# Three fused layers on one core: both heads of a pair normed together, all K and Q casts on ScalarE, a new order

## The chip, the cores and the metric

The kernel runs on one core of a Trainium2 chip. The core has five engines with a queue each, and each works its queue strictly in order: PE (TensorE, matmuls; its weight loads are a row of their own, PEld), DVE (VectorE), ACT (ScalarE), POOL (GpSimd) and SP (which only starts transfers here). PE writes to PSUM, eight banks of 512 float32 columns in each of 128 partitions; DVE and ACT read PSUM, POOL does not. The metric is the device time in microseconds of one execution, and the median over several executions.

## The reference, cut to what matters

Attention over 4 batches, 8 heads, 576 tokens and 64 columns a head, each head's output mixed with a read from a memory matrix, followed by a mixture of experts (8 experts, 288 tokens each) and a last layer of three products and a maximum.

```
scores = q @ k.T / 8, causal mask, softmax with the row's maximum taken off
local  = softmax @ v
mem    = (phi(q) @ M_prev) / (phi(q) @ z_prev + 1e-6)
out    = g * mem + (1 - g) * local          # g = sigmoid(beta), one per head
x      = moe(out)                           # each token to one expert, experts have a capacity
y      = maximum of three x @ w, then @ w_out
```

Everything is float32. The softmax needs the sum of each row's exponentials; the kernel gets it as one more column of the product with v, and divides at the end.

## The kernel before, in words

The attention runs over 16 pairs of heads (four batches of four pairs), numbered from 0 here. For a pair, with K and Q loaded as `Kr` and `Qr`:

- *Casts and differences.* For each head `KX`, `QX` and `KB` are rounded copies of K and Q (`ck`, `cq`, `cb` in `pair`), which the scheduler may give to ACT or to DVE; POOL then subtracts them from the originals in pieces of 192 columns (L84), so that the product of rounded parts and remainders keeps float32 accuracy.
- *S* (L509) and *J* (L511): the scores with the queries in the partitions, only to get the row maximum. DVE reduces each piece (L528). J is the last block of 64 queries of both heads at once. *N* (L562) transposes the maxima, ACT copies them, and three small transfers put them into a row of `QL`.
- *T* (L629, L630): the scores again with the keys in the partitions, now with the maximum taken off, in four groups a head: 512 columns; 64 and 448; 320 and 192; and a 64x64 corner. ACT takes the exponential into `PT` (L640), POOL masks the diagonal blocks (L658).
- *AV* (L675): 15 products a head of `PT` with V, into one PSUM bank per head, `av_109` for the first head of each pair and `av_110` for the second. 73 columns a query block are used: 64 of output, 8 of the head's share of the expert gate, and the row's sum.
- *Norm* (`norm`, L693 to L704), on DVE for each head: the sums times the gate factor (`r`), their reciprocal, the product with the bank (`tmp`), and two additions into `x`, 320 and 40 columns a partition.
- *M* (L724) is the memory product of the pair and *G* (L407) the gate's product with V. Besides, 24 pieces of the last layer's weights are converted from 64-bit halves by ACT and DVE (L869 to L879).

The eight PSUM banks of this stage are two for AV, one for M, G and small products, three for S and two for T. The 64x64 corner of T has no bank of the T ring: it goes to the free columns 448 to 511 of the head's own AV bank, so it is written after the previous owner of that bank has been normed.

Nothing of the order is written by hand. Every step is a task with a key (a place in the program, shifted by the entries of `PRIO`), the engines that may do it with a guessed cost for each, its inputs and its buffers. `Plan.run` then plays the program through with those costs and sets the order in which each engine gets its instructions. The costs (`act`, `dve`, and numbers beside the tasks) are thus no times of the chip, but they decide the order. `FILL` sets 32 matmuls on constant data (L790, `warm`), which have the last key of all and go where PE would otherwise idle at the start; `COLD` is the time before which the planner counts PE's work twice.

After the attention comes the routing of the tokens (a chain of small steps between DVE and PE), and then the experts and the last layer, with a plan of their own.

Of the kernel before, what the change touches and what calls it, by code (L numbers as in the profile page):

```python
# [33 lines left out]
NJ = 5  # L34
# [97 lines left out]
class Plan:  # L132
# [113 lines left out]
def attention(g, tc, ctx, consts, beta, qT, kT, qN, v1, vT, mz, mT, wg, xd, L, m2):  # L246
# [97 lines left out]
    def pair(p):  # L344
# [103 lines left out]
        def head(i):  # L448
# [42 lines left out]
    def maxes(r, p):  # L491
# [5 lines left out]
        def piece(key, heads, j, a, z, first, last, dep):  # L497
# [19 lines left out]
            def fR(e):  # L517
# [4 lines left out]
                if not last:  # L522
# [81 lines left out]
    def unit(r, p, i):  # L604
# [14 lines left out]
        for gi, gr in enumerate(groups):  # L619
            o = K()  # L620
            bt = Buf(R["t"]) if gi < 3 else r.bav[i]

            def fT(e, gr=gr, o=o, gi=gi):
                o.t = ps.tile([128, 512], F32, name="t", bufs=BUFS["t"]) if gi < 3 else AV[h % 2][:, 448:512]
# [23 lines left out]
        for gi, (kb, cnt, st) in enumerate(((0, 2, 576), (2, 2, 320), (4, 1, 64))):  # L648
# [11 lines left out]

            c = {"DVE": dve(cnt * m), "POOL": 40 + 1.25 * cnt * m}
            mk.append(add(n1 + W["M"] + .1 * gi, {x: c[x] for x in W["maske"]}, fM, ex[:2] if gi == 0 else ex[2:3] if gi == 1 else ex[3:],
                          use=[bP]))
        out = []
        for j in range(NJ):
            m = rows(j)

            def fA(e, j=j, m=m):

                av = AV[h % 2][:, j * C:j * C + CA]  # L670
                for kb in range(j + 1):
# [7 lines left out]
                           mk[:1] + (fill if p == 0 else []) + (ex[1:2] if j else []) + (mk[1:2] if j > 1 else []) + (mk[2:] if j > 3 else []) + [r.tV] + out[-1:],  # L679
                           use=[bP, r.b["V"], r.bav[i]]))  # L680
        return out

    def norm(r, p, i, deps, mems):
        b, pp = divmod(p, H // 2)
        h = 2 * pp + i
        n = r.n + 5 * i + 4 + W["norm"]
        av = av3(AV[h % 2])
        u = K()
        br, bt = Buf(R["r5"]), Buf(R["tmp"])

        def f1(e):
            u.r5 = tile("r5", [128, NJ])
            V.tensor_scalar(u.r5, av[:, :, 72], 1.0e-9, g.c1[:, h:h + 1], op0=OP.add, op1=OP.mult)  # L693

        def f2(e):
            V.reciprocal(u.r5, u.r5)

        def f3(e):
            u.tmp = tile("tmp", [128, NJ, 72])
            V.tensor_mul(u.tmp, av[:, :, :72], u.r5[:, :, None].to_broadcast([128, NJ, 72]))  # L700

        def f4(e):
            for x, c0, c1 in ((x2s[b].t[:, :, h], 0, 64), (xs[b][:, :, h], 64, 72)):
                vg(e).tensor_add(x, x, u.tmp[:, :, c0:c1])  # L704

        t = add(n, {"DVE": 130}, f1, deps + [cdone], new=[br], use=[r.bav[i]])
        t = add(n + .1, {"DVE": 100}, f2, [t], use=[br])
        t = add(n + .2, {"DVE": dve(360)}, f3, [t], new=[bt], use=[br, r.bav[i]])
        c = {"POOL": 1020, "DVE": dve(320) + 90}
        return add(n + .3, {x: c[x] for x in (W["xadd"] if p < NP - 1 else ("POOL", "DVE"))}, f4, [t] + mems, use=[bt, r.bx, r.bx2])  # L710

    def mem(r, p, part):
# [30 lines left out]
        def f3(e):  # L743
# [3 lines left out]
            for dst, c0, c1 in ((x2s[b].t, 0, 64), (xs[b], 64, 72)):  # L747
# [74 lines left out]
    for p in range(NP):  # L822
# [24 lines left out]
    def conv(k):  # L847
# [728 lines left out]
```

## Time and profile before

| | us |
|---|---|
| median of 3 runs | 941.97 (934.69 to 942.91) |
| the profiled execution | 938.56, span 936.8 |
| attention, first instruction to the last norm | 0 to 296.5 |
| routing and start of the experts | 296.5 to 360 |
| experts and last layer | 360 to 936.8 |
| busy over the span: PE, DVE, ACT, POOL | 863.9, 570.9, 316.5, 433.6 |

The page is one execution on the chip. A busy PE there is an upper figure, since matmuls are pipelined and their ends are modelled. DMA issues of an engine are not counted as busy. Times in the rows below are us from the start of the span, unless ns is written.

### The profile page before, as it was taken

How to read it: one execution, taken by the hardware profiler on the slowest of the kernel's cores; microseconds unless marked ns; L12 is line 12 of the kernel's file. 1: busy time of each engine (PE TensorE's matmuls, PEld its weight loads, DVE VectorE, ACT ScalarE, POOL GpSimd, SP SyncE). 2: the span in 40 equal slices, each digit the busy share in tenths (PEclk: the TensorE clock that was granted, in tenths of full speed). 3: DMA queues.
4: the chain of work that ended last, by engine and by line, in shares of the span. 5: the costliest groups of instructions: out<-in, count | busy, mean ns of one | idle time of the engine just before them, and what ended most of it. 6: DMA issues, size and time to landing. Idle time of an engine off the chain costs nothing.

```text
span 936.8 us, 17494 instructions
## 1 busy us (share of the span) xinstructions
PE 863.9 (92%) x6493; PEld 788.0 (84%) x6493; DVE 570.9 (61%) x1708; ACT 316.5 (34%) x683; POOL 433.6 (46%) x665
## 2 busy tenths in 40 slices
PE   8999999999997467999989998999999999979997
PEld 5888888888886357989979988989998998979996
DVE  5699999997756864842682683484376386123121
ACT  3445555553334032223124133224223224322211
POOL 1758777677421396344064155136208326730301
PEclk9699999999998569999999999999999999989999
DMA  7456776854201122231042032024014114340000
GB/s 282 164 200 201 252 256 218 281 162 133 94 18 52 54 62 91 72 112 46 2 138 91 2 115 95 21 79 138 23 47 146 38 52 154 116 91 23 24 1 34
DMA packets 37601, 97.86 MB, mean 104 GB/s; under 512 B 9620, under 2 KB 9740, under 8 KB 37516
## 3 DMA queue, kind: packets, MB, share of 16 engines
q1 hardware_dynamic: 34240, 87.24, 28.8%
q0 software_dynamic: 2976, 9.44, 3.0%
q8 instruction: 51, 0.84, 0.4%
q14 instruction: 34, 0.28, 0.1%
q10 hardware_dynamic: 300, 0.07, 0.0%
HBM read 87.22 MB, written 9.45 MB: 103 GB/s over the span
## 4 chain that ended last, share of the span: by engine, by line
PE 61%; DVE 11%; POOL 10%; issue 8%; DMA 8%; ACT 2%; SPq 0%; POOLq 0%; ACTq 0%; DVEq 0%
PE av L675 10%; PE w L1323 7%; PE w L1325 7%; PE w L1324 7%; DMA wraw<-in_wr 5%; PE acc L1325 4%; PE acc L1323 4%; PE acc L1324 4%; POOL ml L84 4%; POOL wlo L84 3%; PE s L509 3%; PE t L629 2%; PE mem L724 2%; PE t L630 2%; PE mem L407 2%
## 5 line engine op out<-in xcount | busy, mean ns | idle before, releaser
L84 POOL TENSOR_TENSOR wlo<-wraw,whi 128x256 fp32r<-128x256 f32 x224 | 167.6, 783 | 253.2 <-ACT whi L1289 251.1
L1323 PE MATMUL w<-yh,mh 128*128 128x288 f32 x576 | 175.1, 304 | 4.8 <-ACT mt L1425 4.8
L1324 PE MATMUL w<-yl,mh 128*128 128x288 f32 x576 | 171.7, 298 | 0.1
L1325 PE MATMUL w<-yh,ml 128*128 128x288 f32 x576 | 171.1, 297 | 0.0
L675 PE MATMUL av<-V,PT 128*128 128x112 f32 (+2 forms) x960 | 130.7, 275 | 0.0
L675 PEld LDWEIGHTS av<-V,PT 128*128 128x128 f32 (+2 forms) x960 | 114.9, 174 | 13.7 <-issue 4.6
L1323 PEld LDWEIGHTS w<-yh,mh 128*128 128x128 f32 x576 | 109.9, 191 | 8.0 <-ACT mt L1425 5.0
L1324 PEld LDWEIGHTS w<-yl,mh 128*128 128x128 f32 x576 | 109.9, 191 | 3.4 <-DVE yl L1229 0.3
L1325 PEld LDWEIGHTS w<-yh,ml 128*128 128x128 f32 x576 | 110.1, 191 | 0.0
L1227 DVE SCALAR_TENSOR_TENSOR hl<-w,hh 128x288 fp32r<-128x288 f32 x64 | 28.8, 456 | 132.3 <-ACT hh L1221 132.3
L1427 DVE TENSOR_TENSOR mt<-w,mt 128x288 f32<-128x288 f32 x96 | 43.5, 453 | 102.9 <-PE w L1325 84.0
L1289 ACT CAST whi<-wraw 128x1024 fp32r<-128x1024 f32 x64 | 67.2, 1049 | 114.9 <-DMA wraw<-in_wr 89.9
L528 DVE CUSTOM_DVE_ANT_0 junk<-s,mask 128x256 bf16<-128x256 f32 (+4 forms) x145 | 72.8, 505 | 23.6 <-PE s L509 19.8
L1325 PE MATMUL w<-xhi,wlo 128*128 128x288 f32 x256 | 77.7, 304 | 8.1 <-DVE wlo L78 7.5
L640 ACT ACTIVATE PT<-t 128x512 f32<-128x512 f32 x96 | 54.5, 594 | 78.7 <-PE av L675 48.7
L1323 PE MATMUL w<-xhi,whi 128*128 128x288 f32 x256 | 78.0, 305 | 1.1 <-ACT whi L1289 1.1
L1324 PE MATMUL acc<-hl,whi 128*128 128x288 f32 x256 | 76.8, 300 | 0.8 <-DVE hl L1227 0.8
L1324 PE MATMUL w<-xlo,whi 128*128 128x288 f32 x256 | 77.1, 301 | 0.0
L1323 PE MATMUL acc<-hh,whi 128*128 128x288 f32 x256 | 77.1, 301 | 0.0
L1325 PE MATMUL acc<-hh,wlo 128*128 128x288 f32 x256 | 76.5, 299 | 0.0
L84 POOL TENSOR_TENSOR KX<-Kr,KX 64x192 fp32r<-64x192 f32 x90 | 63.1, 729 | 21.0 <-ACT KX L312 13.8
L658 POOL TENSOR_SCALAR_AFFINE_SELECT PT<-PT 128x256 f32<-128x256 f32 (+1 forms) x96 | 41.2, 440 | 66.7 <-ACT PT L640 61.2
(236 smaller groups left out, 1925.0 us busy)
## 6 DMA issues: line engine op xcount, KB each, us to landing
wraw<-in_wr SPq DMA_DIRECT2D x64, 512.0 KB
Kr<-in_kT SPq DMA_DIRECT2D x15, 576.0 KB
Qr<-in_qT SPq DMA_DIRECT2D x15, 576.0 KB
V<-in_v SPq DMA_DIRECT2D x16, 384.5 KB
m2raw<-in_m2w SPq DMA_DIRECT2D x12, 512.0 KB
QN<-in_qN SPq DMA_DIRECT2D x16, 288.0 KB
VT<-in_vT SPq DMA_DIRECT2D x16, 288.0 KB
xd<-x SPq DMA_DIRECT2D x16, 256.0 KB
```

Of the source, the lines that this page charges most:

```text
L84: u = nc.gpsimd.tensor_sub(o[:, c], a[:, c], b[:, c])
L509: nc.tensor.matmul(o.s[:, :z - a], r.QX[i][:, 128 * j:128 * j + 128], r.KX[i][:, a:z], start=True, stop=True)
L528: V.tensor_tensor_reduce(out=junk[ps_, :z - a], in0=o.s[ps_, :z - a], in1=mask[ps_, k:k + z - a], scale=-0.125, scalar=init, op0=OP.add, o ...
L640: A.activation(u.PT[:kr, at0:at0 + wd], o.t[:kr, :wd], AF.Exp, scale=0.125)
L658: G.affine_select(v, v, pattern=[[1, m]] if cnt == 1 else [[0, 2], [1, m]], compare_op=OP.is_ge, fill=0.0, base=0, channel_multiplier=-1)
L675: nc.tensor.matmul(av[:m], u.PT[:kr, o:o + m], r.Vw[:kr, c:c + CA], start=(kb == 0), stop=(kb == j))
L1227: V.scalar_tensor_tensor(lo(), src(), 0.0, hi().bitcast(F32), op0=OP.max, op1=OP.subtract)
L1289: A.copy(x.W[fb][0], x.RAW[fb])
L1323: nc.tensor.matmul(o, wh, rh, start=start, stop=False)
L1324: nc.tensor.matmul(o, wh, rl, start=False, stop=False)
L1325: nc.tensor.matmul(o, wl, rh, start=False, stop=stop)
L1427: V.tensor_max(q.mt, o.pt[:, :T], q.mt)
```

## The change

Three things in the attention; the routing, the experts and the last layer keep their code.

1. The two AV banks become one tile of two banks, and the two heads of a pair are normed together after both: five DVE instructions a pair where there were ten, with twice the columns. The two AV banks come free together. The ring of `tmp` goes from three buffers to two. The 64x64 corner of T goes to the T ring like the other groups.
2. From the second pair on, the casts to `KX`, `QX` and `KB` may only go to ACT.
3. The costs that the planner counts with, and several keys, are replaced, with `COLD` from 6000 to 25000; so each engine's order changes through the whole attention.

```diff
-PRIO = {..., 'phi': 2.0, ..., 'cpe': ['ACT', 'DVE'], ..., 'J4': -2.0, 'R': -78.0, ..., 'N': -37.5, 'T': -3.0, ..., 'gate': 45.5, 'G': -13.0, ...}
+PRIO = {..., 'phi': 22.0, ..., 'cpe': ['ACT'], ..., 'J4': 38.0, 'R': -98.0, ..., 'N': -42.5, 'T': -43.0, ..., 'gate': 2.5, 'G': -3.0, ...}
...
-NROW, COLD, NLAT = 1, 6000, 3000
+NROW, COLD, NLAT = 1, 25000, 3000
...
-    AV = [ps.tile([128, 512], F32, name=f"av{i}") for i in range(2)]
+    AVP = ps.tile([128, 2, 512], F32, name="av")
+    AV = [AVP[:, i] for i in range(2)]
...
     def act(n, psum=False):
-        return 22 + 0.89 * n if psum else 60 + 0.89 * n
+        return 135 + 0.89 * n if psum else 155 + 0.89 * n
...
-            bt = Buf(R["t"]) if gi < 3 else r.bav[i]
+            bt = Buf(R["t"])
...
-    def norm(r, p, i, deps, mems):
+    def norm(r, p, deps, mems):
+
         b, pp = divmod(p, H // 2)
-        h = 2 * pp + i
-        n = r.n + 5 * i + 4 + W["norm"]
-        av = av3(AV[h % 2])
+        h = slice(2 * pp, 2 * pp + 2)
+        n = r.n + 9 + W["norm"]
+        av = AVP[:, :, :NJ * C].rearrange("p i (j c) -> p j i c", j=NJ)
...
-            u.tmp = tile("tmp", [128, NJ, 72])
-            V.tensor_mul(u.tmp, av[:, :, :72], u.r5[:, :, None].to_broadcast([128, NJ, 72]))
+            u.tmp = tile("tmp", [128, NJ, 2, 72])
+            V.tensor_mul(u.tmp, av[:, :, :, :72], u.r5[:, :, :, None].to_broadcast([128, NJ, 2, 72]))
...
-        for i in range(2):
-            last = unit(r, p, i)
-            nm.append(norm(r, p, i, last, [m0, m1]))
+        last = unit(r, p, 0) + unit(r, p, 1)
+        r.avs = [r.bav[0], r.bav[1]]
+        nm.append(norm(r, p, last, [m0, m1]))
```

How the order moves, at two places. First ACT near the start, before: `c_120`, `c_121` are small constants, `QL<-t` the maxima of pair 0's first head, and `KX<-Kr` x2 the first casts of pair 1.

```order
L103 ACTIVATE c_120<-bt 128x8
L104 ACTIVATE c_121<-bt 128x8
L312 COPY V<-mem 128x10x8
L312 CAST QL<-t 1x512
L312 CAST QL<-t 1x64
L312 CAST KX<-Kr 128x576 x2
L640 ACTIVATE PT<-t 128x512
```

The casts of pair 1 stand behind three copies that wait for PE. The same place in the changed kernel:

```order
L103 ACTIVATE c_119<-bt 128x8
L104 ACTIVATE c_120<-bt 128x8
L310 CAST KX<-Kr 128x576
L310 CAST KB_126<-Kr 64x576
L310 CAST KX<-Kr 128x576
L310 CAST QX<-Qr 128x576 x2
L310 CAST KB_127<-Kr 64x576
L420 ACTIVATE ph<-QN 128x576
L425 ACTIVATE ph<-ph 128x576
L638 ACTIVATE PT<-t 128x512
```

Now all six casts of pair 1 and its `phi` stand directly behind the constants, and the three copies have gone to DVE.

Second, PE where pair 7 ends and pair 8 begins, before: `av_110` is the bank of a pair's second head, `av_109` that of the next pair's first.

```order
L675 MATMUL av_110<-V,PT 64x112 x5
L509 MATMUL s<-KX,QX 128x128
L675 MATMUL av_109<-V,PT 128x112
L509 MATMUL s<-KX,QX 128x256
L675 MATMUL av_109<-V,PT 128x112 x2
```

One S piece stands between the last product of a pair and the first of the next. The same place in the changed kernel, where both heads write the one tile `av`:

```order
L673 MATMUL av<-V,PT 64x112 x5
L509 MATMUL s<-KX,qj_129 128x512 x2
L509 MATMUL s<-KX,qj_129 128x64 x2
L627 MATMUL t<-QX,KX 128x320
L628 MATMUL t<-QL,KB_125 128x320
L627 MATMUL t<-QX,KX 128x192
L628 MATMUL t<-QL,KB_125 128x192
L627 MATMUL t<-QX,KX 64x64
L628 MATMUL t<-QL,KB_125 64x64
L673 MATMUL av<-V,PT 128x112 x2
```

Four J matmuls and three groups of T now stand between; the corner of T is written to `t`, no longer to the AV bank.

## Rows read from the trace of the kernel before

**Rows 1.** Windows: stretch, its length, busy us (xcount) of PE, PEld, DVE, ACT, POOL, clock, DMA.
```profile
28.00:45.00 17.00, 16.54 (x64) 14.68 (x65) 10.70 (x39) 8.10 (x19) 13.41 (x24) 0.51 0.39 132
...
75.00:200.00 125.00, 122.44 (x889) 106.37 (x888) 119.75 (x388) 66.79 (x143) 95.08 (x145) 1.00 0.72 237
200.00:287.00 87.00, 83.67 (x615) 72.71 (x616) 59.05 (x202) 34.08 (x74) 42.87 (x113) 1.00 0.27 84
```

**Rows 2.** One line's instructions, norm's product: duration ns min/median/max, first and last start.
```profile
L700 DVE TENSOR_TENSOR tmp<-av,r x32: 514/528/534, 49.5 to 295.3; 128x360 f32<-128x360 f32 x32
```

**Rows 3.** The chain that ended last, one pair late in the attention: start, length, what.
```profile
242.43 0.69 DVE junk L528
...
244.65 1.05 issue
245.70 0.58 DVE x L704
```

**Rows 4.** Waits of PE, 60 to 290: waiting, releaser, us in total, times, longest.
```profile
PE s L562 <- DVE nm L528: 3.4, 4, 1.0
```

**Rows 5.** Groups by shape, 0 to 310, norm and M's product: count | busy us, mean ns.
```profile
L704 DVE TENSOR_TENSOR x<-x,tmp 128x320 f32<-128x320 f32 x32 | 21.5, 672 | 0.3
L704 DVE TENSOR_TENSOR x<-x,tmp 128x40 f32<-128x40 f32 x32 | 11.6, 362 | 0.0
L748 DVE TENSOR_TENSOR x<-mem,rm 128x384 f32<-128x384 f32 x16 | 8.7, 547 | 0.2
L693 DVE TENSOR_SCALAR r<-av,c 128x5 f32<-128x5 f32 x32 | 7.1, 221 | 15.5 <-PE av L675 13.4 <-ACT mh L1200 2.0
L748 DVE TENSOR_TENSOR x<-mem,rm 128x256 f32<-128x256 f32 x16 | 6.6, 411 | 0.2
L696 DVE RECIPROCAL r<-r 128x5 f32<-128x5 f32 x32 | 5.9, 184 | 0.2
```

**Rows 6.** The same view: casts of K and Q on DVE, and one kind on ACT.
```profile
L312 ACT CAST QX<-Qr 128x576 fp32r<-128x576 f32 x19 | 12.8, 671 | 5.8 <-PE av L630 3.2 <-PE av L629 2.5
L312 DVE CAST KB<-Kr 64x576 fp32r<-64x576 f32 x19 | 11.3, 595 | 0.5 <-PE av L630 0.5
L312 DVE CAST QX<-Qr 128x576 fp32r<-128x576 f32 x13 | 7.1, 556 | 0.0
L312 DVE CAST KX<-Kr 128x576 fp32r<-128x576 f32 x13 | 6.2, 476 | 0.0
```

**Rows 7.** Timeline: an addition of norm beside POOL's subtraction: start, us, engine.
```profile
227.18 1.94 POOL L84 TENSOR_TENSOR QL<-Qr,QX 64x192 fp32r<-64x192 f32 x3 [0.60 <-PE av L630]
227.22 1.96 DVE L704 TENSOR_TENSOR x<-x,tmp 128x320 f32<-128x320 f32 x2
```

**Rows 8.** Timeline near the start, ACT, then PE.
```profile
18.06 0.19 ACT L104 ACTIVATE c<-bt 128x8 f32<-128x8 f32 x1
...
23.16 1.24 ACT L312 CAST KX<-Kr 128x576 fp32r<-128x576 f32 x2
```

**Rows 9.** Timeline of PE where it first sat idle, with the wait in brackets.
```profile
27.38 0.42 PE L590 MATMUL t<-identr,nmr 128*1 128x128 f32 x4 [1.53 <-DVE nmr L584]
28.46 0.21 PE L592 MATMUL t<-identr,nmr 64*1 64x64 f32 x1 [0.66 <-ACT QL L312]
28.60 1.11 PE L509 MATMUL s<-KX,QX 128*128 128x128 f32 x3
```

**Rows 10.** Timeline of DVE, the last two norms.
```profile
292.42 0.60 DVE L704 TENSOR_TENSOR x<-x,tmp 128x320 f32<-128x320 f32 x2
294.81 0.23 DVE L693 TENSOR_SCALAR r<-av,c 128x5 f32<-128x5 f32 x1 [1.79 <-PE av L675]
...
295.86 0.60 DVE L704 TENSOR_TENSOR x<-x,tmp 128x320 f32<-128x320 f32 x2
```

**Rows 11.** Timeline of PE: two T groups and the corner, then the next head's first.
```profile
282.50 0.39 PE L629 MATMUL t<-QX,KX 128*128 128x320 f32 x1
...
283.18 0.48 PE L629 MATMUL t<-QX,KX 128*128 128x512 f32 x1
```

More of the change, by code (lines that the diff above doesn't have):

```diff
@@ L55 @@
 FK = {"m2": -600, "m2b": -40, "ml": ("POOL",), "load": -30, "wsplit": -12, "wlo": ("POOL",), "gather": -60, "xt": -50, "h1": 0, "y": 3, "o": 6, "store": 57.5, "idx": 35}
-BUFS = {'Kr': 2, 'Qr': 2, 'QN': 2, 'MZ': 2, 'V': 3, 'VT': 2, 'phi': 2, 'ph': 1, 'KX': 6, 'QX': 5, 'QL': 2, 'KB': 4, 'QJ': 3, 'nm': 3, 'nmr': 1, 'n9': 1, 'PT': 2, 's': 3, 't': 2, 'r5': 2, 'tmp': 3, 'rm': 2, 'x': 2, 'm2raw': 2, 'm2a': 1, 'm2b': 1, 'x2': 2}
+BUFS = {'Kr': 2, 'Qr': 2, 'QN': 2, 'MZ': 2, 'V': 3, 'VT': 2, 'phi': 2, 'ph': 1, 'KX': 6, 'QX': 5, 'QL': 2, 'KB': 4, 'QJ': 3, 'nm': 3, 'nmr': 1, 'n9': 1, 'PT': 2, 's': 3, 't': 2, 'r5': 2, 'tmp': 2, 'rm': 2, 'x': 2, 'm2raw': 2, 'm2a': 1, 'm2b': 1, 'x2': 2}
 OFFK = (0, 576, 1024, 1344, 1536)
 ACTX = 0
-PRIO = {'load': -12, 'phi': 2.0, 'min2': ['ACT'], 'prep': 7.5, 'cpe': ['ACT', 'DVE'], 'sube': ['POOL'], 'S': -71.0, 'J4': -2.0, 'R': -78.0, 'E': 29.0, 'N': -37.5, 'T': -3.0, 'A': 18.5, 'M': -60.0, 'rowe': ['ACT'], 'maske': ['POOL'], 'norm': 0.5, 'xadd': ['DVE'], 'mem': [0, 9], 'gate': 45.5, 'G': -13.0, 'gev': ['ACT'], 'm2': [15.0, 4.6, 25.0]}
+PRIO = {'load': -12, 'phi': 22.0, 'min2': ['ACT'], 'prep': 7.5, 'cpe': ['ACT'], 'sube': ['POOL'], 'S': -71.0, 'J4': 38.0, 'R': -98.0, 'E': 29.0, 'N': -42.5, 'T': -43.0, 'A': 18.5, 'M': -60.0, 'rowe': ['ACT'], 'maske': ['POOL'], 'norm': 0.5, 'xadd': ['DVE'], 'mem': [0, 9], 'gate': 2.5, 'G': -3.0, 'gev': ['ACT'], 'm2': [15.0, 4.6, 25.0]}
 C = 73
@@ L436, in pair @@
         a = add(kp + .1, {"ACT": act(S)}, phi2, [a], use=[b_["ph"]])
-        r.tphi = add(kp + .2, {"DVE": dve(S)}, phi3, [a], use=[b_["ph"], b_["phi"], b_["QN"]])
+        r.tphi = add(kp + .2, {"DVE": dve(S) + 140}, phi3, [a], use=[b_["ph"], b_["phi"], b_["QN"]])
         def scale(e):
@@ L475, in head @@
             cp = {x: {"ACT": act(S), "DVE": dve(S, False)}[x] for x in W["cpe"]}
-            sb = {x: {"POOL": 1390, "DVE": dve(S)}[x] for x in W["sube"]}
+            sb = {x: {"POOL": 2050, "DVE": dve(S)}[x] for x in W["sube"]}
             if not p:
-                cp, sb = {"ACT": act(S), "DVE": dve(S, False)}, {"POOL": 1390, "DVE": dve(S)}
+                cp, sb = {"ACT": act(S), "DVE": dve(S, False)}, {"POOL": 2050, "DVE": dve(S)}
             t1 = add(kh, cp, ck, [tK[i]], new=[bh["KX"]], use=[b_["Kr"]])
@@ L532, in piece @@
             new = not ttr
-            ttr.append(add(key + 5 * heads[-1] + W["R"], {"DVE": max(dve(z - a), 196)}, fR, ts + dep, new=[bnm] if new else [],
+            ttr.append(add(key + 5 * heads[-1] + W["R"], {"DVE": 235 + 1.02 * (z - a)}, fR, ts + dep, new=[bnm] if new else [],
                            use=[bs] + ([] if new else [bnm])))
@@ L620, in unit @@
             o = K()
[L621 removed]
+            bt = Buf(R["t"])
             def fT(e, gr=gr, o=o, gi=gi):
[L624 removed]
+                o.t = ps.tile([128, 512], F32, name="t", bufs=BUFS["t"])
                 c = 0
@@ L659, in fM @@
                                     fill=0.0, base=0, channel_multiplier=-1)
-            c = {"DVE": dve(cnt * m), "POOL": 40 + 1.25 * cnt * m}
+            c = {"DVE": dve(cnt * m), "POOL": 150 + 1.4 * cnt * m}
             mk.append(add(n1 + W["M"] + .1 * gi, {x: c[x] for x in W["maske"]}, fM, ex[:2] if gi == 0 else ex[2:3] if gi == 1 else ex[3:],
@@ L698, in f3 @@
         def f3(e):
-            u.tmp = tile("tmp", [128, NJ, 72])
-            V.tensor_mul(u.tmp, av[:, :, :72], u.r5[:, :, None].to_broadcast([128, NJ, 72]))
+            u.tmp = tile("tmp", [128, NJ, 2, 72])
+            V.tensor_mul(u.tmp, av[:, :, :, :72], u.r5[:, :, :, None].to_broadcast([128, NJ, 2, 72]))
         def f4(e):
             for x, c0, c1 in ((x2s[b].t[:, :, h], 0, 64), (xs[b][:, :, h], 64, 72)):
[L704 to L710, printed above, removed]
+                vg(e).tensor_add(x, x, u.tmp[:, :, :, c0:c1])
+        t = add(n, {"DVE": 214}, f1, deps + [cdone], new=[br], use=r.avs)
+        t = add(n + .1, {"DVE": 180}, f2, [t], use=[br])
+        t = add(n + .2, {"DVE": dve(720) + 60}, f3, [t], new=[bt], use=[br] + r.avs)
+        c = {"POOL": 2040, "DVE": 1250}
+        return add(n + .3, {x: c[x] for x in W["xadd"]}, f4, [t] + mems, use=[bt, r.bx, r.bx2])
     def mem(r, p, part):
@@ L751, in mem @@
         t = add(n, {"PE": 251 * k}, f0, [r.tphi, r.tmz], new=[bm], use=[r.b["phi"], r.b["MZ"]])
-        t = add(n + .1, {"DVE": 75}, f1, [t, cdone], new=[br], use=[bm])
-        t = add(n + .2, {"DVE": 80}, f2, [t], use=[br])
-        return add(n + .3, {"DVE": dve(144 * k) + 70}, f3, [t] + ([firsts[b]] if b in firsts else []),
+        t = add(n + .1, {"DVE": 150}, f1, [t, cdone], new=[br], use=[bm])
+        t = add(n + .2, {"DVE": 170}, f2, [t], use=[br])
+        return add(n + .3, {"DVE": dve(144 * k) + 190}, f3, [t] + ([firsts[b]] if b in firsts else []),
                    new=[pend[b], x2s[b].b] if first else [], use=[bm, br] + ([] if first else [pend[b]]))
@@ L883, in conv @@
         t1 = add(n + W["m2"][2], {"ACT": act(512)}, f1, [t0], new=[ba], use=[br])
-        t2 = add(n + W["m2"][2], {"DVE": 335}, f2, [t0], new=[bb], use=[br])
-        t3 = add(n + W["m2"][2] + .1, {"DVE": 602}, f3, [t1, t2], use=[ba, bb])
-        add(n + W["m2"][2] + .2, {"DVE": 602}, f4, [t3], use=[br, bb])
+        t2 = add(n + W["m2"][2], {"DVE": 460}, f2, [t0], new=[bb], use=[br])
+        t3 = add(n + W["m2"][2] + .1, {"DVE": 740}, f3, [t1, t2], use=[ba, bb])
+        add(n + W["m2"][2] + .2, {"DVE": 740}, f4, [t3], use=[br, bb])
     for k in range(24):
```

8 lines of the change are left out of this document (3 added, 5 removed).

## The prediction

> **What bounds the kernel now.** I read the windows first, to find the stretches that the change can touch; then the spacing of one instruction that comes once a head, for the pace; then the chain of waits, for what sets that pace; then the groups by shape, for prices; the timeline only where two engines meet.
>
> The change leaves the routing, the experts and the last layer alone, so all that follows concerns the first 297 us. Norm's product runs 32 times from 49.5 to 295.3 us, 31 steps of 7.93 us, so a pair takes 15.86 us [rows 2]. In the windows the reader is to compare PE with DVE [rows 1]. From 75 to 200 us PE is busy 122.44 of 125 us and DVE 119.75: both full, PE a little more so. From 200 to 287 us DVE has dropped to 59.05 of 87, because the weight conversions are through, and PE is still at 83.67; yet the pace is no better. So DVE's load by itself doesn't set the pace there. The chain tells what costs a little there: a reduction of S, a gap, and norm's addition one after another on DVE [rows 3], while PE waits for the maxima, 3.4 us in four waits [rows 4]. ACT is half idle throughout, 66.79 of 125 us [rows 1], though its DMA issues come on top.
>
> **The change part by part.** Every price is of the one profiled execution, 938.56 us; its place among the runs comes at the end.
>
> *DVE's relief.* Counting both orders, DVE loses 19 casts to KB, 12 to QX and 11 to KX (some remain in pair 0): 19 x 0.595 + 12 x 0.556 + 11 x 0.476 = 23.2 us [rows 6]. Norm costs now, a pair, 2 x (0.221 + 0.184 + 0.528 + 0.672 + 0.362) = 3.93 us [rows 2, 5]. For the merged form I need a price per column: M's product goes from 0.411 to 0.547 us for 128 columns more, 1.06 ns a column [rows 5]. So r 0.23, reciprocal 0.19, product 0.528 + 0.38 = 0.91, additions 0.672 + 0.34 = 1.01 and 0.362 + 0.04 = 0.40, together 2.74 us: 1.19 us less a pair, 19 us over 16 pairs. Together DVE has 42 us less to do, 2.6 us a pair.
>
> *What ACT gets.* The same 42 casts at 0.67 us, 28 us [rows 6], less ten small copies that go to POOL. In 75 to 200 us (7.9 pairs) that is some 14 us more, 81 of 125: it is hidden under PE as long as exponentials don't arrive late for it. Costed at nothing; without that cover it is the second rival.
>
> [...] The row is 0.671 us for a cast on ACT against 0.476 to 0.595 on DVE [rows 6]. [...]
>
> *The steady stretch, 75 to 287 us.* PE's matmuls are the same in number and size, so what can be gained is what PE loses to waits. The rows bound it. At the low end it is PE's visible idle time, 125 - 122.44 + 87 - 83.67 = 5.9 us, and nothing at all if the new order only moves the waits. At the high end DVE alone sets the pace to 200 us, and 2.6 us a pair over 7.9 pairs gives 20.5 us, while the idle time after 200 us (3.3) goes too: 24 us. I take 9 us, nearer the low end, since PE's row is the fuller of the two; the 3 us over 5.9 are for waits that the modelled matmul ends cover up.
>
> *The start.* Pair 1's first casts start at 23.16 us on ACT though its constants end at 18.25 [rows 8]; in the new order nothing that waits for PE stands between. K has long been issued, and its landing bounds this: between 0 and 4.9 us earlier. After the idle time at 25.8 to 28.6 us, PE starts pair 1's S at 28.60 [rows 9], so it can use them. I take 3 us. [...]
>
> *The pair's end.* Next pair's first AV product now waits for the product of the merged norm. [...] At the thinnest boundary three T groups cover 283.18 - 282.50 = 0.68 us [rows 11] and four J matmuls lie before them; at most others all of the next T and S pieces lie between. Behind that AV stand T and S of the pairs after, which ACT and DVE wait for. I take 0.3 us in all, between nothing and 15 x 0.9 = 14 us. The corner of T no longer waits for the norm; it now takes its turn in the ring of two, behind ACT's exponential (0.67 us at most): costed at nothing, since two such waits a pair go and two come.
>
> *The end.* The last norm was 294.81 to 296.46 us [rows 10]; merged, it is longer by 0.01 + 0.01 + 0.38 + 0.38 = 0.8 us, and nothing covers it, because the routing waits for its sum. The gate's reductions only move earlier for three batches.
>
> *The DMA queue.* The loads of the next pairs wait for the casts and POOL's differences of a pair two before; they are issued in nearly the same sequence, and DMA is at 0.72 [rows 1]; nothing.
>
> Sum: -9 - 3 + 0.3 + 0.8 = -10.9, so 927.7 us against 938.56. That execution lies 3.4 us under the median of 941.97 but inside the runs' range; half of that is added: **929 us**.
>
> **The rivals.**
>
> *PE is full already.* PE busy 98% of 75 to 200 us says so [rows 1]; against it, PE's figure is an upper one, and PE has visible waits on DVE [rows 4]. Or ACT takes DVE's place: casts of 0.67 us before each exponential, so that T waits for its buffers. At 0.35 us for each of 26 heads that is 9 us, the whole gain. Either way the time stays at about 938 to 940. The change then moves its cost and doesn't do what it is made for.
>
> *The merged tile stalls PE.* The place is the first AV of each pair. DVE works in order, and what stands ahead of r can be held up: an addition took 1.96 us beside POOL's subtraction [rows 7] and 0.60 alone [rows 10]. If the queue is late by that 1.4 us beyond the cover at each of 15 boundaries and the new casts' delay of 0.67 adds up behind it, PE loses about 1.9 x 15 = 28 us, less 10.9 gained: +17, or 957 us. It decides where DVE reaches r over a microsecond after the last AV; so far DVE is mostly idle there, 13.4 us of waits for AV [rows 5]. That speaks against.
>
> *Fewer collisions.* The addition of [rows 7] ends with POOL's last piece, at 229.18 and 229.12. If POOL holds DVE off in this manner in each pair after 200 us, the chain of [rows 3] loses 1.36 us once for each of 5.5 pairs by halving the number of additions, 7 us beyond the forecast: 922 us. [...]
>
> [...]
>
> **How the numbers follow.** Forecast 0.44, with its own range 921 to 935 from the bounds (24 us for the steady stretch is its far end, 4 its near one); fewer collisions 0.05; clock 0.05; PE or ACT full 0.36; merged tile 0.10. A measurement of this kernel tells a change of over 1% (9.4 us) from none. Faster by that, under 932.5: the forecast less 0.02, and the two small ones, 0.52. Within 1%: 0.38. Slower: 0.10. The range leaves out the stalls and the far end of the fast cases; above it ends where the first rival stands if it comes out at the median of the runs, 942, and half of their spread of 8.2 us: 917 to 946 us.
>
> **What would show it.** Right: the spacing of norm's product falls from 15.86 us a pair to about 15.2; DVE's busy time to 200 us falls by some 15 us or more; ACT's rises by as much and no wait of PE for an exponential grows; pair 1's first cast starts before 19.5 us. Wrong: PE waiting for DVE at the first AV of a pair (the merged tile), or T waiting for ACT (its casts), or an unchanged spacing with DVE at 80% (PE was full). [...]

## The result and the profile after

| | before | after |
|---|---|---|
| median of the first runs, us | 940.43 (4 runs) | 927.95 (4 runs) |
| ratio, 95% interval | | 0.9875 (0.9833 to 0.9917) |
| the same, measured again on another chip | 941.33 (23 runs) | 932.67 (12 runs) |
| ratio, 95% interval | | 0.9926 (0.9894 to 0.9959) |
| profiled execution, span | 936.8 | 926.7 |
| end of the last norm's product in it | 295.8 | 282.2 |
| from there to the end of the span | 641.0 | 644.4 |

The forecast was 929 us. The change gains about 1%, 9 to 12 us; in the profiles the attention ends 13.6 us earlier. The ratios compare only the fast runs of each kernel, so they are not the quotients of the medians above them.

Windows of the changed kernel, the columns of [rows 1], and one stretch more:

```profile
0.00:75.00 75.00, 71.00 (x471) 58.19 (x472) 57.00 (x197) 43.10 (x90) 43.26 (x89) 1.00 0.66 229
28.00:45.00 17.00, 17.00 (x121) 13.91 (x119) 11.11 (x45) 8.12 (x18) 10.62 (x20) 1.00 0.46 156
...
75.00:200.00 125.00, 123.94 (x910) 108.77 (x909) 95.59 (x311) 74.74 (x155) 81.09 (x154) 1.00 0.67 217
200.00:287.00 87.00, 81.53 (x604) 71.00 (x602) 55.38 (x183) 45.25 (x89) 38.13 (x103) 0.98 0.34 112
```

The first stretch in the kernel before, and the fillers alone in the changed kernel (us, count, clock, DMA):

```profile
0.00:75.00 75.00, 68.97 (x413) 56.24 (x414) 56.06 (x187) 33.80 (x77) 39.48 (x74) 0.89 0.61 214
```

```profile
28.00:45.00 17.00, 1.77 (x8) 1.00 0.46 156
```

Read the counts of PE. From 28 to 45 us PE does 121 matmuls where it did 64 [rows 1], at a clock of 1.00 instead of 0.51. Eight of the 121 are fillers, of which the kernel before had run all 32 by 28 us, so these 17 us gain 49 of the matmuls that do the work. Counted from the start to 75 us, with the fillers through in both, it is 471 against 413: 58 matmuls ahead, of which the 9 outside those 17 us were gained before them. (In the second profiles of both kernels, below, it is 463 against 415.) At 125 / 889 = 0.141 us a matmul 58 are 8.2 us. From 75 to 200 us the lead grows by 910 - 889 = 21 matmuls, 3.0 us. The last norm is 0.7 us longer (below), so 13.6 + 0.7 - 8.2 - 3.0 = 3.1 us come after 200 us. Matmuls differ in length, so these shares are estimates. The 24 us that DVE is lighter from 75 to 200 us (119.75 to 95.59) show up in the pace as 3 us.

Waits of PE, 60 to 281 us, the columns of [rows 4]:

```profile
PE av L673 <- DVE tmp L699: 0.8, 1, 0.8
PE s L507 <- ACT PT L638: 0.2, 1, 0.2
```

That is all that is left, 1.0 us. The kernel before waited 6.0 us in that stretch: the maxima of [rows 4], 0.5 us more for maxima, 0.9 for a mask of POOL, and T for an exponential:

```profile
PE t L629 <- ACT PT L640: 1.2, 1, 1.2
```

The waits for the maxima are gone, T waits for no exponential, and the merged tile is waited for once in 15 boundaries.

Three of the four waits of [rows 4] come from the collision of [rows 7], which is there again at 244 and 261 us: each time the last reduction of S stands behind the held-up additions on DVE, and PE waits for its maxima. One of the three, on POOL, DVE and PE:

```profile
244.27 1.95 POOL L84 TENSOR_TENSOR QL<-Qr,QX 64x192 fp32r<-64x192 f32 x3 [0.60 <-PE av L630]
244.32 1.96 DVE L704 TENSOR_TENSOR x<-x,tmp 128x320 f32<-128x320 f32 x2
246.54 0.28 PE L562 MATMUL s<-ident,nm 128*9 128x128 f32 x1 [1.03 <-DVE nm L528]
```

The three waits are 3.1 us together, as much as the lead that comes after 200 us. In the changed kernel one pair of additions takes 1.37 us there and the others 0.97 to 1.19, and PE waits for none of them.

Groups by shape up to 310 us, for [rows 5, 6]:

```profile
L692 DVE SCALAR_TENSOR_TENSOR r<-av,c 128x10 f32<-128x10 f32 x16 | 2.7, 168 | 21.5 <-PE av L673 21.5
L695 DVE RECIPROCAL r<-r 128x10 f32<-128x10 f32 x16 | 3.4, 213 | 0.1
L699 DVE TENSOR_TENSOR tmp<-av,r 128x720 f32<-128x720 f32 x16 | 14.5, 903 | 0.1
L703 DVE TENSOR_TENSOR x<-x,tmp 128x640 f32<-128x640 f32 x16 | 13.5, 844 | 0.1
L703 DVE TENSOR_TENSOR x<-x,tmp 128x80 f32<-128x80 f32 x16 | 6.6, 411 | 0.0
...
L310 ACT CAST KB<-Kr 64x576 fp32r<-64x576 f32 x32 | 21.3, 666 | 17.4 <-DMA Kr<-in_kT 5.6 <-DMA QL<-n 5.3 <-PE t L628 5.1
```

The merged norm costs 0.17 + 0.21 + 0.90 + 0.84 + 0.41 = 2.54 us a pair; 2.74 was forecast, from 3.93. Over the attention DVE is busy 36 us less (241.55 in the first 298 us, 205.20 in the first 284); 42 was forecast.

PE at the start (start, us, instruction), for [rows 9], and the first casts of pair 1 on ACT, for [rows 8]:

```profile
25.11 0.68 PE L507 MATMUL s<-KX,QX 128*128 128x512 f32 x1
25.64 0.58 PE L588 MATMUL t<-identr,nmr 128*1 128x128 f32 x4
...
28.13 0.39 PE L627 MATMUL t<-QX,KX 128*128 128x512 f32 x1
```

```profile
16.72 0.67 ACT L310 CAST KX<-Kr 128x576 fp32r<-128x576 f32 x1 [1.10 <-DMA Kr<-in_kT]
17.29 0.67 ACT L310 CAST KB<-Kr 64x576 fp32r<-64x576 f32 x1
```

The transposes follow without a gap where before PE sat idle for 1.53 and 0.66 us. A matmul of 512 columns takes 0.68 us just ahead of them and 0.39 at 28.13; I call these the lower and the upper level. T's products with `KX` take up to 0.72 us before 28 us, and at most 0.51 from there to the last at 273.5 us: PE stays at the upper level to the end of the attention. Ahead of the transposes it was still at the lower level, so the level comes up here; it doesn't merely fail to fall. The first cast comes 6.4 us earlier than at 23.16 and now waits for nothing but the landing of K.

DVE at the last norm, for [rows 10]:

```profile
280.87 0.17 DVE L692 SCALAR_TENSOR_TENSOR r<-av,c 128x10 f32<-128x10 f32 x1 [6.12 <-PE av L673]
...
281.33 0.91 DVE L699 TENSOR_TENSOR tmp<-av,r 128x720 f32<-128x720 f32 x1
282.27 0.98 DVE L703 TENSOR_TENSOR x<-x,tmp 128x640 f32<-128x640 f32 x2
```

From r to the last addition it is 2.38 us, before 1.65: 0.73 longer, where 0.8 was forecast.

### The profile page after: what moved, and what is told of

It reads as the page before. It is cut to its first block, busy times and chain, and to the rows that moved or that the text cites. A ratio compares the mean times of both kernels' runs of the same rounds, so it can differ in the third digit from the quotient of the medians.

```text
span 926.7 us, 17359 instructions
## 1 busy us (share of the span) xinstructions
PE 857.0 (92%) x6493; PEld 783.6 (85%) x6493; DVE 533.8 (58%) x1587; ACT 335.4 (36%) x713; POOL 418.2 (45%) x676
## 4 chain that ended last, share of the span: by engine, by line
PE 66%; DVE 10%; POOL 9%; issue 7%; DMA 5%; ACT 2%; ACTq 0%; SPq 0%; POOLq 0%; DVEq 0%
PE av L673 12%; PE w L1322 8%; PE w L1324 7%; PE w L1323 7%; DMA wraw<-in_wr 5%; PE acc L1324 4%; PE acc L1322 4%; PE acc L1323 4%; POOL ml L84 4%; POOL wlo L84 3%; PE s L507 3%; PE t L627 3%; PE t L628 3%; PE mem L723 2%; PE mem L405 2%
## 5 line engine op out<-in xcount | busy, mean ns | idle before, releaser
L673 PE MATMUL av<-V,PT 128*128 128x112 f32 (+2 forms) x960 | 127.9, 275 | 0.8 <-DVE tmp L699 0.8
L673 PEld LDWEIGHTS av<-V,PT 128*128 128x128 f32 (+2 forms) x960 | 111.1, 173 | 13.6 <-issue 3.1
L526 DVE CUSTOM_DVE_ANT_0 junk<-s,mask 128x256 bf16<-128x256 f32 (+3 forms) x145 | 73.2, 508 | 32.9 <-PE s L507 28.0
L638 ACT ACTIVATE PT<-t 128x512 f32<-128x512 f32 (+1 forms) x128 | 61.2, 498 | 68.4 <-PE av L673 31.5
L656 POOL TENSOR_SCALAR_AFFINE_SELECT PT<-PT 128x256 f32<-128x256 f32 (+1 forms) x96 | 38.2, 408 | 73.3 <-ACT PT L638 67.2
L84 POOL TENSOR_TENSOR KX<-Kr,KX 64x192 fp32r<-64x192 f32 x90 | 56.4, 654 | 11.9 <-ACT KX L310 9.0
```

Source lines behind the costliest of these rows:

```text
L84: u = nc.gpsimd.tensor_sub(o[:, c], a[:, c], b[:, c])
L526: V.tensor_tensor_reduce(out=junk[ps_, :z - a], in0=o.s[ps_, :z - a], in1=mask[ps_, k:k + z - a], scale=-0.125, scalar=init, op0=OP.add, o ...
L638: A.activation(u.PT[:kr, at0:at0 + wd], o.t[:kr, :wd], AF.Exp, scale=0.125)
L656: G.affine_select(v, v, pattern=[[1, m]] if cnt == 1 else [[0, 2], [1, m]], compare_op=OP.is_ge, fill=0.0, base=0, channel_multiplier=-1)
L673: nc.tensor.matmul(av[:m], u.PT[:kr, o:o + m], r.Vw[:kr, c:c + CA], start=(kb == 0), stop=(kb == j))
```

## The experiments

The theory from this profile: the start gains because PE never sits idle near 26 us, so its clock is not low from 28 to 45 us; the rest comes from waits that the new order removes; DVE's load sets no pace by itself. Rivals: DVE's relief sets the pace; the earlier casts make the start; ACT's casts cost something. Each kernel has two measures here: the ratio of its times to the kernel before on the same chip, and the end of the last norm's product in its profile, which is not blurred by the experts behind it (636.6 to 650.2 us in the profiles of all kernels that leave the code there as it is).

**The kernel before, gaps filled**

```diff
+                for k in range(9 * i):
+                    nc.tensor.matmul(AV[1][:, :FILL[1]], warm[:, :128], warm[:, :FILL[1]], start=True, stop=True)
...
+                for k in range(4 * i):
+                    nc.tensor.matmul(AV[1][:, :FILL[1]], warm[:, :128], warm[:, :FILL[1]], start=True, stop=True)
```

`FILL[1]` is 384. The first nine stand ahead of the second head's transposes, the four ahead of the last of them.

> The kernel before, same order on every engine, with 13 more matmuls on constant data (384 columns each) in the two gaps of PE near 26 and 28 us. Clock theory: the changed kernel's gain at the start came from PE never sitting idle there. Then the granted clock stays at 1.00 from 28 to 45 us here too, PE does its 16.5 busy us of that stretch in half the time, and the time falls by about 8 us, to 0.991 of the kernel before. Rival, the changed kernel gained there because pair 1's casts come earlier: the fillers only fill dead time, 0 to 1 us, ratio 1.000.

> The kernel before with 13 fillers in PE's two gaps near 26 and 28 us, timed again, since its profile had the last norm's product 4 to 5 us earlier and its 12 times no gain to speak of (0.9993, interval 0.9952 to 1.0034). Theory: the upper level from 26 us on is worth what the profile shows, 0.994 to 0.997. Rival: other executions lose it elsewhere, 0.999 to 1.001.

PE in the first of the two profiles:

```profile
26.39 1.82 PE L590 MATMUL av<-warm 128*128 128x384 f32 x9
28.05 0.41 PE L592 MATMUL t<-identr,nmr 128*1 128x128 f32 x4
...
31.43 0.45 PE L633 MATMUL t<-QX,KX 128*128 128x512 f32 x1
```

No gap, and the 512 columns of T take 0.45 us. The clock reads 1.00 from 28 to 45 us in both profiles, and 111 and 109 matmuls are done there (six and four of them fillers) instead of 64: 41 more that do work, 5.8 us, of the changed kernel's 49. Neither its earlier casts nor its order is needed for these; the rest is left to them. The last norm's product ends at 291.6 and 291.5 us, 4.2 us earlier than in the first profile of the kernel before. That is the mechanism as the theory has it, but less than 8 us: other waits come in at once (a cast's difference on POOL, 1.2 us, a reduction, 0.6). The times show less still: 0.9993 (0.9952 to 1.0034) and 0.9978 (0.9940 to 1.0017). The 0.991 that the theory expected at first lies outside both. Both allow 4 us and neither shows it, so what the level is worth in the median stays open between nothing and some 5 us.

**The kernel before, profiled again**

> The kernel before, profiled a second time. If the fall of the clock near 28 us comes from PE's two gaps there, it is there again, from about 28 to 45 us, and the last norm's product ends within 2 us of 295.8. If it strikes by chance, it stands elsewhere or nowhere, and the attention ends some 5 us earlier.

```profile
25.88 0.72 PE L629 MATMUL t<-QX,KX 128*128 128x448 f32 x1
...
27.37 0.59 PE L590 MATMUL t<-identr,nmr 128*1 128x128 f32 x4 [0.23 <-ACT qj L312]
28.62 0.21 PE L592 MATMUL t<-identr,nmr 64*1 64x64 f32 x1 [0.66 <-ACT QL L312]
...
32.63 0.73 PE L629 MATMUL t<-QX,KX 128*128 128x512 f32 x1
```

The slow stretch is there again: 0.73 us for 512 columns, 66 matmuls from 28 to 45 us, the last norm's product at 296.8. Here the recorded clock reads 1.00 all through it. It is not a fall, though. The 448 columns take 0.72 us at 25.88, before the gaps, so PE is at the lower level already and stays there; in the first profile the same product took 0.45 us, so there the level had come up and fell:

```profile
25.09 0.45 PE L629 MATMUL t<-QX,KX 128*128 128x448 f32 x1
```

Either way PE is low to 44 or 45 us after waits near 28 us (a clock of 0.50 to 44 us in the first profile, 66 matmuls in these 17 us in the second); what keeps it low so long is not shown. The duration of one kind of matmul tells the level, the record not always: here it reads 1.00 beside 0.73 us.

**The changed kernel with a gap put in**

```diff
+                for k in range(4 * i):
+                    w = slice(0, 512)
+                    V.tensor_reduce(spare, mask[:, w], axis=AX.X, op=OP.add)
                 u.nr = tile("nmr", [128, 9], F32R)
+                if i:
+                    V.tensor_copy(u.nr[:, :1], spare[:, :1])
```

> The changed kernel with four idle reductions of 512 columns on DVE ahead of the copy that PE's transposes near 25.6 us wait for, which should make PE idle for about 2 us there. Clock theory: the clock falls to 0.50 for some 17 us after it, and the time rises by the gap and 8 us, to about 938 us. Rival, the clock has nothing to do with it: at most the 2 us of the gap, 930 us.

```profile
25.24 0.68 PE L508 MATMUL s<-KX,QX 128*128 128x512 f32 x1
28.21 0.59 PE L594 MATMUL t<-identr,nmr 128*1 128x128 f32 x4 [2.29 <-DVE nmr L588]
...
30.91 0.63 PE L633 MATMUL t<-QX,KX 128*128 128x512 f32 x1
```

0.9962 (0.9930 to 0.9995), 934.87 us. PE sits idle for 2.29 us, and the 512 columns still take 0.63 us at 30.91; the upper level comes at about 34 us instead of 28 (23 matmuls in the 6 us from 28 to 34, 79 in the 11 from 34 to 45). The last norm's product ends at 286.6, 4.4 us later, 2.1 more than the gap. So in the profile the rival "only the gap" falls, but so does my 8 us: here the gap delays a rise by 6 us instead of undoing one for 17. The time decides nothing, since its interval overlaps that of the changed kernel's second measurement.

The code alone, further below, has such a gap too, and the clock behind it reads:

```profile
27.21 0.91 PE L723 MATMUL mem<-MZ,phi 128*128 128x146 f32 x4 [1.20 <-DVE x L747]
```

```profile
28.00:38.00 10.00, 10.00 (x50) 8.08 (x50) 5.62 (x24) 4.88 (x13) 6.00 (x13) 0.50 0.68 229
```

Over all profiles: in the ten in which PE doesn't wait between 26 and 29 us it does 109 to 121 matmuls from 28 to 45 us; in the four in which it does, 64 and 66 (the kernel before), 101 (this one) and 101 (the code alone).

**The changed kernel with two norms a pair, everything else in place**

```diff
-            V.tensor_mul(u.tmp, av[:, :, :, :72], u.r5[:, :, :, None].to_broadcast([128, NJ, 2, 72]))
+            for i in range(2):
+                V.tensor_mul(u.tmp[:, :, i], av[:, :, i, :72], u.r5[:, :, i, None].to_broadcast([128, NJ, 72]))
```

(r, reciprocal and additions likewise.)

> The changed kernel with the same order, tiles and buffers, but the five instructions of each norm done per head as ten: 1.39 us more of DVE for each of 16 pairs, 22 us. DVE theory (its relief sets the pace): PE waits more and the time rises by 3 us or more, to 931 to 937 us. PE theory (PE was full and DVE's load is off the path): within 2 us of 928, of which the last norm takes 1.4.

```profile
75.00:200.00 125.00, 123.45 (x905) 108.10 (x903) 99.13 (x351) 74.12 (x153) 79.39 (x152) 1.00 0.65 217
```

0.9908 (0.9873 to 0.9942), 928.35 us, the last norm's product at 283.2: no measurable loss, 905 matmuls against 910. DVE's busy time rises by only 6.5 us over the first 284, not by the 16.6 that the durations of the ten instructions here have over those of the five, since neighbours overlap (in the changed kernel the last two additions, 0.84 and 0.41 us on average, are through in 0.98). The saving of the merged norm's instructions is worth nothing that could be measured.

**The changed kernel with 42 casts back on DVE**

```diff
-                copy(e, r.KB[i][:64], r.Kr[:64, i])
+                copy("DVE" if p else e, r.KB[i][:64], r.Kr[:64, i])
...
-                copy(e, r.QX[i], r.Qr[:, i])
+                copy("DVE" if p > 3 and not i else e, r.QX[i], r.Qr[:, i])
```

> The changed kernel with 42 casts (all KB from pair 1 on, and QX of each first head from pair 4 on) moved back from ACT to DVE, at the same place of the program: DVE has about 24 us more to do, ACT 28 us less. DVE theory: 932 to 940 us, with PE waiting for DVE. PE theory: within 2 us of 928. ACT theory (the casts on ACT held exponentials up): 2 to 5 us faster than the changed kernel.

```profile
168.94 0.67 PE L673 MATMUL av<-V,PT 128*128 128x112 f32 x4 [0.85 <-DVE tmp L699]
170.19 0.38 PE L560 MATMUL s<-ident,nm 128*9 128x128 f32 x1 [0.58 <-DVE nm L526]
...
172.08 0.63 PE L628 MATMUL t<-QL,KB 65*128 65x512 f32 x1
```

0.9966 (0.9932 to 1.0000), 933.1 us; the last norm's product at 288.8, 6.6 us late. DVE has become late at one boundary: PE waits 0.85 us for the merged norm, 0.58 for the maxima, and then 512 columns take 0.63 us; the clock reads 0.61 from 168 to 176. DVE is still only 102.53 of 125 us busy from 75 to 200 us. From 155 to 200 us PE does 301 matmuls, the changed kernel 325, so about half of the loss is here (24 matmuls, 3.4 us); another 6 to 14 were missing by 75 us already (457; the changed kernel had 471 and 463). So in the profile the casts matter less by DVE's mean load than by when the late instruction meets PE; no cost of ACT's casts is seen. By the times the loss is less sure: the interval overlaps that of the changed kernel's second measurement.

**The order alone, the code alone, and steps between**

First: the kernel before with the changed kernel's costs, keys and `COLD`, casts still free. Second: the changed code with the old ones. The planner works out each order anew from these numbers, so neither kernel has another's order instruction by instruction.

```diff
-PRIO = {..., 'cpe': ['ACT', 'DVE'], ..., 'J4': -2.0, 'R': -78.0, ..., 'N': -37.5, 'T': -3.0, ...}
+PRIO = {..., 'cpe': ['ACT', 'DVE'], ..., 'J4': 38.0, 'R': -98.0, ..., 'N': -42.5, 'T': -43.0, ...}
...
-NROW, COLD, NLAT = 1, 6000, 3000
+NROW, COLD, NLAT = 1, 25000, 3000
```

> The kernel before (a bank and a norm for each head, casts on ACT or DVE as the planner likes, 41 of them on DVE) with the changed kernel's costs, keys and COLD: the order alone. Theory: the order gives the gain at the start (7.6 us at equal work of PE) and most of the rest, and DVE's relief only 2 to 3 us (what 24 us more casts on DVE cost the changed kernel in the steady stretch): 0.990 to 0.993 of the kernel before, the last norm's product near 286 us. Rival, merged norm and casts on ACT make the gain: 0.998 to 1.002, near 294 us.

> The changed kernel's code (one tile for both heads, merged norm, casts on ACT) planned with the costs, keys and COLD of before. Theory (the order makes the gain): within 4 us of the kernel before, 0.996 to 1.002, the last norm's product at 291 to 296 us. Rival (DVE's relief makes it): 0.986 to 0.990, near 283 us.

Both are slower than the kernel before: 1.0183 (1.0133 to 1.0233), 957.73 us, and 1.0121 (1.0081 to 1.0162), 952.05 us. Neither theory nor rival had that. The order alone: two instructions of PE with the wait ahead of them, and the window around them:

```profile
159.25 1.83 PE L724 MATMUL mem<-MZ,phi 128*128 128x146 f32 x6 [2.05 <-DVE x L748]
161.78 0.32 PE L629 MATMUL av<-QX,KX 128*64 128x64 f32 x1 [0.70 <-DVE tmp L700]
```

```profile
155.00:175.00 20.00, 16.06 (x88) 13.42 (x87) 13.16 (x47) 7.91 (x16) 8.21 (x14) 0.74 0.42 144
```

It is level with the changed kernel up to 155 us; then PE waits for DVE at M's product and at the corner, and does 88 matmuls in 20 us at a clock of 0.74. The code alone: its longest sums of waits from 20 to 298 us, and one of them in the timeline of PE:

```profile
PE t L627 <- ACT PT L638: 4.7, 9, 1.0
PE s L507 <- ACT QX L310: 2.7, 3, 1.3
```

```profile
88.66 0.50 PE L627 MATMUL t<-QX,KX 128*128 128x512 f32 x1 [1.04 <-ACT PT L638]
```

Here it is ACT. I read it so that the casts stand in its queue at places that suit the old sharing, which is argued and not shown; after 1.04 us without work the clock reads 0.50 from 90 to 96 us. This is the rival "ACT takes DVE's place", and it is real under the old order.

Then the order with the corner of T in the T ring, and that with all casts on ACT as well:

```diff
-            bt = Buf(R["t"]) if gi < 3 else r.bav[i]
+            bt = Buf(R["t"])
...
-'cpe': ['ACT', 'DVE']
+'cpe': ['ACT']                       # second of the two only
```

> The order alone as before (a bank and a norm for each head, casts free, 37 on DVE), with one thing more of the change: the 64x64 corner of T goes to the T ring. The order alone showed PE waiting at the corner for norm's product (3.7 us) and at M's product for DVE's addition (6.3 us), and falls of the clock behind such waits. Theory: the new keys put T early, and only with the corner off the AV bank can PE follow them: the waits for tmp go and the falls with them, 0.990 to 1.000 of the kernel before, the last norm's product at 284 to 294 us. Rival: DVE, late by its casts, holds PE all the same at M's product: 1.010 to 1.018, 300 us or more.

> The order and the corner as in the run before last but two, and now the casts from pair 1 on all on ACT too; what is left of the change is the merged norm with its one tile. The kernels with the new order and casts on DVE kept the changed kernel's pace to 155 us, then PE waited 1 to 2 us for DVE and fell to half its clock. Theory: it is the casts in DVE's queue that made it late; without them the pace holds to the end, 0.987 to 0.994 of the kernel before, the last norm's product at 282 to 287 us. Rival: the ten instructions of two norms are late all the same, 1.005 or more, 295 us or later.

1.0157 (1.0104 to 1.0211) and 1.0120 (1.0078 to 1.0162). Windows of the first, then of the second, and PE in the second where it lost the pace:

```profile
75.00:155.00 80.00, 79.67 (x590) 70.27 (x590) 59.67 (x210) 44.07 (x95) 54.83 (x105) 1.00 0.62 208
155.00:200.00 45.00, 40.55 (x227) 33.87 (x228) 34.52 (x114) 17.07 (x35) 19.11 (x36) 0.81 0.51 167
```

```profile
155.00:200.00 45.00, 45.00 (x336) 39.09 (x335) 33.73 (x115) 24.88 (x53) 27.64 (x52) 1.00 0.68 227
200.00:230.00 30.00, 24.88 (x131) 20.68 (x131) 19.91 (x69) 12.39 (x26) 13.36 (x24) 0.77 0.41 130
```

```profile
209.34 0.65 PE L509 MATMUL s<-KX,QX 128*128 128x128 f32 x3 [1.94 <-ACT QX L312]
211.47 0.76 PE L509 MATMUL s<-KX,QX 128*128 128x512 f32 x1 [1.48 <-POOL PT L658]
```

Up to 155 us the first does 590 matmuls in 80 us and the changed kernel 587 (before: 572): with ten norm instructions a pair, and some of the casts on DVE. Then it breaks: 227 matmuls in 45 us. With the casts on ACT it holds to 200 us (336 in 45, changed kernel 325) and breaks at 209, this time on a cast and a mask. My theory that DVE's casts alone make the break is at most half right: with them on ACT, in an order planned anew, that break is gone and another comes. Each planned order has its own weak place; the full change is the one of the five here without any.

**The changed kernel, PE kept busy in the routing**

```diff
+    def hot(n):
+        for _ in range(n):
+            nc.tensor.matmul(rps[:, 272:400], g.ones, g.ones, start=True, stop=True)
...
+                        hot(0 if ph or a0 else 12)    # ahead of each count of the first round
```

> The changed kernel with matmuls on constant data (128 columns each) ahead of the waits of the first round of the routing: 56 before the transpose, 8 before the next product, 12 before each of seven counts, 56 and 64 before the two long waits. If idle gaps are what takes PE to the lower level, as at the start, the level stays up from 282 to 311 us, the 18 matmuls of a count take less than 0.86 us, and the routing is 3 to 5 us shorter: 0.983 to 0.988 of the kernel before. Rival: the level falls all the same, the fillers run at half the speed into the waits and cost 0.3 us a count: 2 us slower than the changed kernel.

```profile
287.22 0.83 PE L977 MATMUL rps<-ones 128*128 128x128 bf16 x12 [0.25 <-DVE am L1011]
...
290.01 0.16 PE L1072 MATMUL rps<-low,ones 1*128 1x8 bf16 x1 [0.93 <-DVE fl L1067]
...
290.63 1.44 PE L977 MATMUL rps<-ones 128*128 128x128 bf16 x12 [0.43 <-DVE n L1082]
```

0.9977 (0.9940 to 1.0015), 935.53 us: no gain over the changed kernel, and behind the last norm's product its profile takes 655.5 us, 11 more. PE from 287 us on: the level falls all the same, after a gap of 0.93 and one of 0.43 us. 12 fillers take 1.44 us at 290.63 where they took 0.83 at 287.22, and each count now comes late behind them. The rival was right.

**The changed kernel again**

> The changed kernel itself, on the chip of the next three runs, so that they have it to stand beside. Expected 0.9875 of the kernel before, as measured, and a second profile in which the last norm's product ends near 282 us and PE stays at the upper level from about 28 us to the end of the attention.

0.9926, as in the table. In its profile the last norm's product ends at 283.3 us, PE does 115 matmuls from 28 to 45 us (the first profile 121, the kernel before 64 and 66), and 907 from 75 to 200.

## Why the prediction was right, and where not

The time was right and its parts were not; that 929 us lies 1 us from the first median (and 4 from the second) is in part luck. I had 5 us too little at the start and 3 too much in the steady stretch, and 3.4 us of what the profile gained didn't reach the end of its span. By the steps of the prediction, in the profiled executions:

- *The start*: -3 us forecast (0 to 4.9), -8.2 found. This is the step that failed. The cast came 6.4 us earlier, more than my bound of 4.9, but I read PE's gaps as a place to be filled. They were worth more for what they did to the clock: 49 of the 58 matmuls gained come where the level had been low. I gave the clock a chance of 0.05, though the new order itself takes away what the idle transposes waited for. Half of the 17 us at a clock of 0.51 [rows 1], 8.5 us, would be too high a price in its turn: with the gaps filled the kernel before does 41 matmuls more there, 5.8 us. Filling the gaps alone moves the end of the attention by 4.2 us, putting one in costs 4.4.
- *The steady stretch*: -9 forecast (0 to 24), -6.1 found. The lower bound, PE's visible idle time of 5.9 us, was nearly exact, and PE's waits fell from 6.0 to 1.0 us; the 3 us that I added for hidden waits, and the upper bound by DVE's load, were not there. The unmerged norm shows it: the same pace without that relief. Half of it is the three waits behind collisions, 3.1 us. The kernel with two norms a pair lacks these waits too, so the number of additions is not what removed them; whether the order, the casts or the tile did, no run isolates. (24 us at the far end would have given 914 us, not the 921 that I wrote as the end of that range.)
- *The merged tile*: +0.3 forecast, one wait of 0.8 us. No run shows the 0.9 us that its upper bound takes for a boundary: from the last AV to the end of the product it is 1.4 us (280.83 to 282.24), 0.7 more than the cover of 0.68 [rows 11], and PE waits at only one boundary of 15. The stall that the rival of the merged tile needs appears once the casts stand in DVE's queue (0.85 us, and a clock of 0.61 from 168 to 176 us), as that rival described it. Its price was added wrongly: 1.4 and 0.67 are 2.07 us a boundary and 31 us in all, not 28.
- *The end*: +0.8 forecast, 0.73 found.
- *ACT's casts at nothing*: right in this order (0.2 us of waits), wrong in the old one (7.4).
- *Fewer collisions*: left out of the sum and a rival at 0.05, worth 7 us; it came, with 3.1 us, inside the steady stretch. The collision was there (in the kernel before three pairs of additions of 1.95 and 1.96 us, each ending 0.06 us after POOL's subtraction), the condition was not: the waits go without halving the number of additions.
- *Behind the attention*: nothing forecast, 3.4 us longer in the first pair of profiles, 7.5 in the second (636.9 and 644.4), 640.0 and 647.0 in two profiles of one and the same kernel. That scatter is as large as the difference, so whether part of the gain is lost there is open; the sum of the other terms, -13.6, is more than either median shows.

Of the signs that I named, to 200 us, DVE's fall (23 us), ACT's rise (17 us), the early cast and the missing waits came. The spacing of norm's product was a bad sign: 281.3 - 46.7 (its last and first start) over 15 is 15.64 us a pair, not 15.2, because in the new order pair 0 is through much earlier than its place in the pace. Matmuls done by a given time, or in a stretch, tell the pace better.

## What to carry to other kernels

Where an engine with a planned order is full, look for its gaps before its load: a gap of one or two us on PE costs itself and, where the clock is lower behind it, about as much again (2.29 us put in, 4.4 lost; 1.4 us of waits at 168 us, 3.4 lost). These are costs in profiles; the medians show them weakly or not at all. Look in the same way at what holds up the one instruction that PE waits for: three collisions of additions cost 3.1 us. Relief of an engine that is busy but not late bought nothing here; the second set of norm instructions was free, and the casts mattered most at the one boundary where DVE came late. And an order fitted to one set of instructions is not a part that can be carried over: order and code lost 1.8 and 1.2% apart and won 1% together.

## What the runs showed of the hardware

- The recorded clock can read 1.00 over a stretch in which 512 columns take 0.73 us instead of 0.45 (the kernel before, second profile). Durations of one shape settle it: by them the changed kernel is at the lower level at 25.11 us (0.68 us), where the record reads 1.00 as well.
- The length of a gap alone did not decide whether the level fell: it fell after 1.04 us (the code alone, 88 us) and after 0.85 and 0.58 us in short succession, and stayed up after the 1.2 us wait of the kernel before, whose next 448 columns take 0.45 us:

```profile
89.01 0.30 PE L629 MATMUL t<-QX,KX 128*128 128x64 f32 x1 [1.16 <-ACT PT L640]
...
89.26 0.45 PE L629 MATMUL t<-QX,KX 128*128 128x448 f32 x1
```

- What decides it is not shown. Behind the inserted gap of 2.29 us, which came while PE was still at the lower level (0.68 us at 25.24), the rise came at about 34 us instead of 28.
- Two additions of norm on DVE took 1.96 us beside POOL's subtraction (244.32) and 0.60 alone [rows 10]; the first profile of the kernel before has this three times after 200 us, with a wait of PE of 1.0 us each. PE's waits for maxima at that line are four in its second profile and in the second of the filled kernel too, 3.3 and 3.4 us together, 1.0 the longest.
- Neighbours on ACT overlap: casts of 0.67 us start 0.57 us apart (16.72 and 17.29). A sum of durations is then too high; 42 casts moved to DVE raised its busy time over the first 284 us by 15.7 us, not by the 24.5 that their durations give there (30 x 0.544 + 12 x 0.683).
